# A kernel of attention and experts: the search's constants in two streams, and one more expert's first layer by seven products of sums

## The chip, the cores and the metric

One core of a Trainium2 chip runs the whole program. The time is the core's device time in microseconds for one execution, as the median of three runs. Everything is float32 unless the code says otherwise.

## The reference

The first half is a linear attention with decay (4 batches, 8 heads, 768 steps, 48 columns a head). Its output, 3072 rows of 384, goes to a mixture of eight experts in which each expert takes exactly 384 rows.

```python
for t in range(S):
    kt, vt, rt = (k[:, :, t], v[:, :, t], r[:, :, t])
    cur = np.einsum('bhd,bhe->bhde', u[None] * kt, vt)
    y[:, :, t] = np.einsum('bhd,bhde->bhe', rt, state + cur)
    state = w[None, :, :, None] * state + np.einsum('bhd,bhe->bhde', kt, vt)
...
logits = x @ w_gate
flat = logits.flatten()
order = np.argsort(-flat)
for idx in order:
    tok, e = (int(idx) // E, int(idx) % E)
    if assigned[tok] >= 0 or counts[e] >= cap:
        continue
    assigned[tok] = e
    counts[e] += 1
...
    h = np.maximum(x[mask] @ w1[e], 0.0)
    out[mask] = h @ w2[e]
```

w1 of an expert is 384 x 1024, w2 is 1024 x 384.

## The kernel before, in words

**Attention** (`Mild`). A unit is 128 steps of one batch; there are 24, four batches a chunk. Units are worked in an order written out by hand in `Mild.run`: in the turn of unit n, PE multiplies the pairs of unit n + 1, turns k and r of unit n + 2 (`kT_ps`, `rT_ps`, line 460) and makes the outputs of unit n (`y_ps`, line 547). VectorE sums `rk` into `dd` (450), scales r (479) and copies the masked pairs into `AT` (514). ACT writes the diagonal of `AT` from `dd` (497, eight writes a unit), copies the outputs out (`x`, 566) and the transposed rows (`xr`, 606). GpSimd multiplies the keys (438) and `rk` (444, 445) and decays the state (532). Each fourth unit also makes the gate's logits. Every engine takes its instructions strictly in the order in which they were written.

**The constants.** The search for the experts' rows needs some twenty small tables. `Assignment.constants` is a generator that issues one instruction a step, GpSimd's and VectorE's mixed, in the order in which the text stands. `Mild.run` takes six steps of it behind each unit from n = 3 on and the rest, if any, behind unit 13. `iota_i`, `own_i`, `number_i` and `by_digit` are written by GpSimd and read by VectorE in the next steps. `digit_15`, `digits`, `steps` and `top` are read only by `surely`, the search that is used in the other arm of the branch at line 2051, which is for inputs that the fast search could not settle.

**The search.** For each expert in turn `likely_steps` finds, with three rounds of counts, the threshold and the rows. A round is a chain between two engines: VectorE writes `ind`, PE counts (978), VectorE writes `own`, `cnt` and `wide`, PE adds up with `ones_h` (989), VectorE reads `most`. After the third, `acc` marks the rows, PE adds them up (`st_ps`, 1105), VectorE makes `place`, `row`, `oh` and `vals`, PE lists (`some_ps` 1450, `list_ps` 1469), and `tok` names the rows. GpSimd then gathers them (1558) and SP loads w1 and w2 of that expert (1551). The search of one expert runs beside the products of the expert two before it, and its small products stand among the large ones in PE's order.

**The experts.** In `Experts.run` an expert is two layers. The expert numbered 0 takes 256 rows early, under the end of attention; 1 to 7 take 384 rows each, and a last turn the remaining 128. The first layer is either plain (`hidden`, `h_ps` at line 1683: 8 blocks of F by 3 of D, 384 columns a product) or by seven (`hidden_by_seven`, line 1660: the 2 x 2 blocks of the first 256 columns of x and of w1 by seven products of sums, with the products of the last 128 columns added in the same banks; 192 columns a product). By seven needs four sums of w1 (`weight_sums`, `first_T`, line 1607), five of the rows (`row_sums`, `first_S`, line 1618) and six additions of kept products (`kept_P`, 1652). The weight sums are made beside the expert before, issued after its first sum `S`; the row sums after the search's `acc`. There is one buffer for each sum. Second layers of experts 1 to 5 are by seven over two thirds of the rows (`seven`, `pa_ps`, `pb_ps`, `pc_ps`, line 1757, with S sums of the hidden rows and T sums of w2 at 1732) and plain over the rest (`o_ps`, 1818); those of 6 and 7 are by fifteen products. Every product in float32 is two passes on PE, and the trace counts passes.

In this part the order on each engine is made by the compiler's scheduler from its own costs, not by hand, so that an added instruction moves others.

Of the kernel before, what the change touches and what calls it, by code (L numbers as in the profile page):

```python
# [13 lines left out]
I32 = mybir.dt.int32  # L14
# [4 lines left out]
ALU = mybir.AluOpType  # L19
AX = mybir.AxisListType  # L20
PSUM = bass.MemoryType.PSUM

NEG = -3.4028234663852886e38
# [253 lines left out]
class Mild:  # L277
# [343 lines left out]
    def run(self, step):  # L621
# [38 lines left out]
        for n in range(N):  # L660
# [66 lines left out]
            if n > 2:  # L727
                for _ in range(6):
                    next(chores, None)
# [8 lines left out]
class Assignment:  # L738
# [24 lines left out]
    def __init__(self, ctx, tc, ML, CAP, C):  # L763
# [22 lines left out]
        new("iota", [128, 128])  # L786
# [14 lines left out]
        new("iota_lo", [128, 128], I32)  # L801
# [23 lines left out]
    def constants(self):  # L825
        nc = self.nc
        NT, E, ND, G, LO = self.NT, self.E, self.ND, self.G, self.LO
        nc.gpsimd.memset(self.ones, 1.0)
        yield
        nc.gpsimd.memset(self.ones_h, 1.0)  # L830
        yield

        nc.gpsimd.memset(self.rest_of, -1.0)
        yield
        nc.gpsimd.affine_select(out=self.rest_of, in_=self.rest_of, compare_op=ALU.is_ge, fill=0.0,
                                base=0, pattern=[[-1, 128]], channel_multiplier=1)
        yield
        nc.gpsimd.memset(self.ones_t, 1.0)
        yield
        nc.gpsimd.memset(self.neg, NEG)  # L840
        yield


        nc.gpsimd.memset(self.by_digit, 1.0)
        yield
        for sign in (1, -1):
            nc.gpsimd.affine_select(out=self.by_digit, in_=self.by_digit, compare_op=ALU.is_ge, fill=0.0, base=0,
                                    pattern=[[-G * sign, ND], [-sign, G]], channel_multiplier=sign)
            yield
        with nc.allow_low_precision(reason="zero or one"):  # L850
            nc.vector.tensor_reduce(out=self.digit_of[:, :, 0], in_=self.by_digit, axis=AX.X, op=ALU.add)
        yield
        nc.vector.tensor_copy(self.digit_of[:, :, 1:E], self.digit_of[:, :, 0:1].to_broadcast([128, ND, E - 1]))
        yield
        nc.vector.tensor_reduce(out=self.same, in_=self.by_digit.rearrange("p d g -> p g d"), axis=AX.X, op=ALU.add)
        yield
        for g in range(3):
            nc.gpsimd.iota(self.from_digit[:, g], pattern=[[ND ** (2 - g), ND], [0, G]],
                           base=(ND ** 2 - ND ** 3, ND, 0)[g], channel_multiplier=0)
            yield  # L860
        Q, NC = 128 // LO, self.CAP // 128
        nc.gpsimd.iota(self.lo_of, pattern=[[1, LO], [0, Q]], base=0, channel_multiplier=0)
        yield
        nc.gpsimd.iota(self.hi_of, pattern=[[1, NC * Q], [0, Q]], base=Q, channel_multiplier=0)
        yield
        nc.vector.tensor_copy(self.digit_15, self.digit_of)
        yield
        nc.vector.memset(self.digit_15[:, ND - 1:ND, :], 0.0)
        yield

        nc.gpsimd.memset(self.quarter, 1.0)
        yield
        for sign, base in ((1, 0), (-1, LO - 1)):
            nc.gpsimd.affine_select(out=self.quarter, in_=self.quarter, compare_op=ALU.is_ge, fill=0.0, base=base,
                                    pattern=[[-LO * sign, Q]], channel_multiplier=sign)
            yield

        nc.gpsimd.iota(self.iota_i, pattern=[[1, 128]], base=0, channel_multiplier=0)
        yield
        nc.vector.tensor_copy(self.iota, self.iota_i)  # L880
        yield
        nc.gpsimd.iota(self.own_i, pattern=[[0, 1]], base=0, channel_multiplier=1)
        yield
        nc.vector.tensor_single_scalar(out=self.own_q, in_=self.own_i, scalar=Q - 1, op=ALU.bitwise_and)
        yield
        nc.vector.tensor_copy(self.own_lo, self.own_q)
        yield
        nc.vector.tensor_scalar(out=self.fourth, in0=self.iota[:, 0:Q], scalar1=self.own_lo, scalar2=None,
                                op0=ALU.is_equal)
        yield  # L890
        nc.vector.tensor_single_scalar(out=self.own_q, in_=self.own_i, scalar=Q.bit_length() - 1,
                                       op=ALU.arith_shift_right)
        yield
        nc.vector.tensor_copy(self.own_lo, self.own_q)
        yield
        nc.vector.tensor_single_scalar(out=self.iota_lo, in_=self.iota_i, scalar=LO - 1, op=ALU.bitwise_and)
        yield
        nc.vector.tensor_scalar(out=self.alike, in0=self.iota_lo, scalar1=self.own_lo, scalar2=None, op0=ALU.is_equal)
        yield
        nc.vector.tensor_scalar(out=self.first_e, in0=self.iota[:, 0:E], scalar1=-1.0, scalar2=float(E),  # L900
                                op0=ALU.mult, op1=ALU.add)
        yield
        nc.vector.tensor_copy(self.first_b, self.first_e)
        yield

        nc.gpsimd.iota(self.number_i, pattern=[[128, NT]], base=-64 * NT, channel_multiplier=1)
        yield
        nc.vector.tensor_copy(self.number, self.number_i)
        yield

        nc.gpsimd.iota(self.digits, pattern=[[1, ND]], base=1, channel_multiplier=0)
        yield
        for g in range(8):
            nc.vector.tensor_single_scalar(out=self.steps[:, g, :], in_=self.digits, scalar=28 - 4 * g,
                                           op=ALU.logical_shift_left)
            yield
# [3 lines left out]
        yield  # L920
        nc.vector.tensor_single_scalar(out=self.top[:, 7:ND - 1], in_=self.steps[:, 0, 7:ND - 1],
                                       scalar=-2147483648, op=ALU.bitwise_xor)
        yield
        nc.vector.tensor_copy(self.top[:, ND - 1:ND], self.top[:, ND - 2:ND - 1])
        yield
        nc.gpsimd.memset(self.taken, 0.0)
        yield
        nc.gpsimd.memset(self.star_place, 0)
        yield
        nc.gpsimd.memset(self.last, float(E * (E - 1) // 2))  # L930
        yield
# [560 lines left out]
def rwkv5_eagle_then_base_layer_balanced(  # L1492
# [34 lines left out]
    class Experts:  # L1527
# [299 lines left out]
        FIRST_BY_SEVEN = 3, 6, 7  # L1827
# [269 lines left out]
```

## Time and profile before

| | us |
|---|---|
| median of 3 runs | 389.97 (389.80 to 390.12) |
| the profiled execution | 389.62 |
| its span, first to last instruction | 387.9 |
| PE busy | 371.6 |
| VectorE (DVE) busy | 268.2 |
| ACT busy | 187.1 |
| GpSimd (POOL) busy | 142.2 |
| first layer of expert 2, plain, starts | 186.4 |
| first layer of expert 3, by seven, starts | 218.0 |

PE is busy for 96% of the span and its granted clock is 0.989 over the whole. In rows of the timeline the first number is the start, the second the length, then the engine, the line, the operation and the tiles (out<-in), the shapes and how many were merged; in brackets stands the idle time of the engine before it and who ended it. PE's rows merge passes of one form, and their lengths contain the modelled drain, so rates are taken from one start to the next.

### The profile page before, as it was taken

The page shows a single profiled execution, that of the slowest core. Times are in us where ns is not written, and L with a number is a line of the kernel's source. Part 1 is how long each engine was busy: PE and PEld are TensorE (multiplying, and loading weights), DVE is VectorE, ACT ScalarE, POOL GpSimd, SP SyncE. Part 2 cuts the span into 40 slices and gives each one's busy share as a digit, 9 for nine tenths or more (in the row PEclk, how much of TensorE's full clock was granted, in tenths as well). Part 3 has the DMA queues.
Part 4 walks back from the last instruction along what each step waited for, and adds up shares of the span by engine and source line. Part 5 has one row for each costly group of instructions (what it writes and reads, how often), then busy time and mean ns, then how long its engine had stood idle before and what let it go on. Part 6 is the DMA issues. An engine that isn't in the chain of part 4 may idle for free. (4 is left out here: it accounts for less than half of the span.)

```text
span 387.9 us, 9795 instructions
## 1 busy us (share of the span) xinstructions
PE 371.6 (96%) x3729; PEld 300.7 (78%) x3729; DVE 268.2 (69%) x940; ACT 187.1 (48%) x468; POOL 142.2 (37%) x175
## 2 busy tenths in 40 slices
PE   7799999999999999999999999999999999999992
PEld 5677878888887775778569799658756889989991
DVE  6655777666887568877649948869367964995530
ACT  4898879888885312225223544322222535535220
POOL 7878877867762005032121221202202322060030
PEclk9899999999999999999999999999999999999997
DMA  7969977777593236473382770408308564690110
GB/s 147 208 133 198 199 165 167 170 169 160 121 327 90 98 130 275 129 280 81 95 333 55 169 285 22 103 0 293 134 23 291 175 235 192 84 365 22 24 63 28
DMA packets 108136, 60.51 MB, mean 156 GB/s; under 512 B 90032, under 2 KB 102320, under 8 KB 108080
## 3 DMA queue, kind: packets, MB, share of 16 engines
q1 hardware_dynamic: 104736, 50.35, 47.5%
q0 software_dynamic: 3104, 9.44, 6.5%
q8 instruction: 31, 0.51, 0.6%
q14 instruction: 25, 0.20, 0.2%
q10 hardware_dynamic: 240, 0.00, 0.0%
HBM read 47.20 MB, written 9.44 MB: 146 GB/s over the span
## 5 line engine op out<-in xcount | busy, mean ns | idle before, releaser
L1683 PE MATMUL h_ps<-xT,w 128*128 128x384 f32 (+1 forms) x264 | 72.7, 427 | 0.0
L497 ACT ACTIVATE AT<-ident,dd 128x128 f32<-128x128 f32 x192 | 59.6, 392 | 4.5 <-DVE dd L450 4.5
L1683 PEld LDWEIGHTS h_ps<-xT,w 128*128 128x128 f32 x264 | 42.0, 191 | 19.7 <-issue 2.3
L1812 POOL DMA_INDIRECT out_dram<-o_all,to x16 | 21.1, 1318 | 92.2 <-DVE o_all L1800 41.0
L1558 POOL DMA_INDIRECT xg<-x_rows,tok x22 | 22.1, 1006 | 84.1 <-DVE own_c L1484 32.7
L1686 ACT ACTIVATE hid<-h_ps 128x384 f32<-128x384 f32 (+1 forms) x40 | 17.9, 448 | 54.8 <-PE h_ps L1683 51.5
L514 DVE COPY_PREDICATED AT<-mask,g_ps 64x512 f32<-64x512 uint8 (+1 forms) x48 | 32.4, 724 | 9.7 <-PE g_ps L507 9.2
L1818 PE MATMUL o_ps<-w,hid 128*128 128x384 f32 x96 | 33.3, 491 | 0.2 <-DVE o_all L1747 0.2
L438 POOL TENSOR_TENSOR kss<-krs,wk 128x384 f32<-128x384 f32 x24 | 24.3, 1014 | 11.6 <-DVE krs L342 7.4
L507 PE MATMUL g_ps<-rT,kT 48*64 48x128 f32 (+1 forms) x768 | 26.9, 258 | 1.4 <-DVE AT L514 0.7
L547 PE MATMUL y_ps<-AT,vts 128*64 128x128 f32 x384 | 26.6, 282 | 0.0
L1818 PEld LDWEIGHTS o_ps<-w,hid 128*128 128x128 f32 x96 | 17.5, 190 | 10.3 <-DVE o_all L1747 0.5
L445 POOL TENSOR_TENSOR rk<-rk,u_bc 128x384 f32<-128x384 f32 x24 | 24.1, 1005 | 1.9
L507 PEld LDWEIGHTS g_ps<-rT,kT 48*64 48x64 f32 x768 | 21.0, 134 | 4.7 <-PE unread_ps L420 0.9
L444 POOL TENSOR_TENSOR rk<-krs 128x384 f32<-128x384 f32 x24 | 24.5, 1021 | 0.0
L547 PEld LDWEIGHTS y_ps<-AT,vts 128*64 128x64 f32 x384 | 21.3, 141 | 1.2 <-issue 0.5
L450 DVE TENSOR_REDUCE dd<-rk 128x8 f32<-128x384 f32 x24 | 13.1, 545 | 7.3 <-POOL rk L445 7.2
L479 DVE TENSOR_TENSOR rT<-rT_ps,WR 112x512 f32<-112x512 f32 x23 | 15.7, 681 | 2.4 <-PE rT_ps L460 2.4
L566 ACT COPY x<-y_ps 128x512 f32<-128x512 f32 x24 | 14.0, 585 | 5.9 <-PE y_ps L547 5.0
L1648 ACT ACTIVATE hid<-kept_P 128x384 f32<-128x384 f32 x18 | 9.4, 523 | 15.2 <-DVE kept_P L1652 14.9
L460 PE MATMUL rT_ps<-ident,krs 128*112 128x128 f32 x96 | 14.9, 274 | 0.7 <-ACT krs L346 0.7
L1757 PE MATMUL pa_ps<-T,S 128*128 128x192 f32 x80 | 15.5, 331 | 0.0
(346 smaller groups left out, 828.9 us busy)
## 6 DMA issues: line engine op xcount, KB each, us to landing
w<-in_moe_w_dram SPq DMA_DIRECT2D x18, 1536.0 KB, 8.6
krs<-in_k_dram SPq DMA_DIRECT2D x24, 192.0 KB, 3.5
krs<-in_r_dram SPq DMA_DIRECT2D x24, 192.0 KB, 3.7
vts<-in_v_dram SPq DMA_DIRECT2D x24, 192.0 KB, 3.6
x_rows<-xr SPq DMA_DIRECT2D x24, 192.0 KB, 2.5
xg<-x_rows,tok POOLq DMA_INDIRECT x22, 4.3
xg<-xg SPq DMA_TRANSPOSE x16, 2.8
out_dram<-o_all,to POOLq DMA_INDIRECT x16, 3.0
```

The costliest lines, as they stand in the source:

```text
L438: self.nc.gpsimd.tensor_mul(self.kss[:, n % self.NS].rearrange("p (g h) d -> p g h d", g=2)[:, :, :, 0:D], src, self.wk.rearrange("p (g h) ...
L444: nc.gpsimd.tensor_mul(rk, self.krs[:, n % self.NK, 1, 0:H, 0:D], self.krs[:, n % self.NK, 0, 0:H, 0:D])
L445: nc.gpsimd.tensor_mul(rk, rk, self.u_bc)
L497: nc.scalar.mul(AT[:, z, a, :], self.ident, dd[:, h:h + 1])
L507: nc.tensor.matmul(g_ps[ts(i, PD), z, a, i * PD:], kT[rows, a, ts(i, PD)], rT[rows, a, i * PD:], start=True, stop=True)
L514: nc.vector.copy_predicated(out=AT[keys, :, :, steps], mask=mask, data=g_ps[keys, :, :, steps])
L547: nc.tensor.matmul(yv[q * PD:(q + 1) * PD, o // 2, o % 2, :], lhsT, rhs, start=(o // 2, q) not in seen, stop=stop, skip_group_check=True)
L1558: nc.gpsimd.indirect_dma_start(out=xg[:, c, :], out_offset=None, in_=x_dram[0:within, :], in_offset=bass.IndirectOffsetOnAxis(ap=tok[:, c: ...
L1683: nc.tensor.matmul(h_ps[j][:, at], w1[:, f, ts(j, 128)], xT[:, f, at], start=(f == 0), stop=(f == KD - 1))
L1686: self.copied = nc.scalar.activation(hid[:, j, 0:m], h_ps[j][:, 0:m], AF.Relu)
L1812: nc.gpsimd.indirect_dma_start(out=to, out_offset=bass.IndirectOffsetOnAxis(ap=tok, axis=0), in_=o_sb, in_offset=None)
L1818: nc.tensor.matmul(o_ps, hid[:, j, ts(c, 128)], w2[:, j, :], start=(j == 0), stop=(j == KF - 1))
```

## The change

The constants become two generators, `by_gpsimd` and `by_vector`. `constants` takes six steps of GpSimd's alone, and from then on one of each in every step. GpSimd's order starts with what VectorE reads. `Mild.run` takes four steps behind a unit instead of six. `digit_15`, `digits`, `steps` and `top` are made in `general_constants`, which `restart` calls at the start of the other arm. `iota` is 8 columns instead of 128, and `iota_lo` is written over `iota_i`. Second, expert 2 joins the experts whose first layer is by seven.

```diff
@@ Mild.run
             if n > 2:
-                for _ in range(6):
+                for _ in range(4):
                     next(chores, None)
@@ Assignment
-        new("iota", [128, 128])
+        new("iota", [128, E])
...
-        new("iota_lo", [128, 128], I32)
     def constants(self):
+        first, then = self.by_gpsimd(), self.by_vector()
+        for _ in range(6):
+            yield next(first)
+        while True:
+            done = [next(part, self) is self for part in (then, first)]
+            if all(done):
+                return
+            yield
+
+    def by_gpsimd(self):
...
+        yield nc.gpsimd.iota(self.iota_i, pattern=[[1, 128]], base=0, channel_multiplier=0)
+        yield nc.gpsimd.iota(self.own_i, pattern=[[0, 1]], base=0, channel_multiplier=1)
+        yield nc.gpsimd.memset(self.by_digit, 1.0)
         for sign in (1, -1):
...
+        yield nc.gpsimd.iota(self.number_i, pattern=[[128, NT]], base=-64 * NT, channel_multiplier=1)
...
+    def by_vector(self):
...
+        yield nc.vector.tensor_copy(self.iota, self.iota_i[:, 0:E])
+        yield nc.vector.tensor_single_scalar(out=self.own_q, in_=self.own_i, scalar=Q - 1, op=ALU.bitwise_and)
...
+    def general_constants(self):
+        nc, E, ND = self.nc, self.E, self.ND
         nc.vector.tensor_copy(self.digit_15, self.digit_of)
-        yield
         nc.vector.memset(self.digit_15[:, ND - 1:ND, :], 0.0)
...
         nc.gpsimd.iota(self.digits, pattern=[[1, ND]], base=1, channel_multiplier=0)
-        yield
         for g in range(8):
             nc.vector.tensor_single_scalar(out=self.steps[:, g, :], in_=self.digits, scalar=28 - 4 * g,
                                            op=ALU.logical_shift_left)
-            yield
...
     def restart(self):
+        self.general_constants()
@@ Experts
-        FIRST_BY_SEVEN = 3, 6, 7
+        FIRST_BY_SEVEN = 2, 3, 6, 7
```

How the instructions stand on the engines, at the places of which the prediction speaks (rows of before with its lines, rows of the change with the lines of the changed text):

VectorE in attention, before, at the end of unit 6's turn: `digit` is the copy that is read only in the other arm, `iota_i` GpSimd's table, `dd` the row sum for ACT.

```order
L531 TENSOR_TENSOR states<-states,kv_ps 128x4x48
L868 MEMSET digit_71 128x4
L880 CAST iota<-iota_i 128x128
L342 COPY krs<-krs 128x2x48
L450 TENSOR_REDUCE dd<-rk 128x8
L479 TENSOR_TENSOR rT<-rT_ps,WR 112x512
```

And now, in the same place:

```order
L531 TENSOR_TENSOR states<-states,kv_ps 128x4x48
L877 TENSOR_SCALAR iota_i<-iota_i 128x128
L878 TENSOR_SCALAR alike<-iota_i,own_lo 128x128
L880 TENSOR_SCALAR first_e<-iota 128x8
L882 CAST first_b<-first_e 128x8
L342 COPY krs<-krs 128x2x48
L450 TENSOR_REDUCE dd<-rk 128x8
L479 TENSOR_TENSOR rT<-rT_ps,WR 112x512
```

The copy of `iota` has moved two turns up, and GpSimd's `iota_i`, which stood in the turn of the reader, is now the first constant behind unit 3.

VectorE in the second layer of expert 1, before: `em` belongs to the search, S are sums of the hidden rows, `own`, `cnt` and `wide` the search's answer to a count.

```order
L1075 TENSOR_REDUCE em<-eq 128x24
L1732 TENSOR_TENSOR S_3154<-hid 128x512
L1732 TENSOR_TENSOR S_3156<-S_3154,hid 128x512
L955 TENSOR_TENSOR own<-counts,same 128x64
L1732 TENSOR_TENSOR S_3158<-hid,S_3156 128x512
L986 TENSOR_REDUCE cnt<-own 128x8
L1747 TENSOR_TENSOR o_all<-kept_P_3167,pc_ps 128x192
L955 TENSOR_TENSOR wide<-digit_of,cnt 128x128
```

And now:

```order
L1047 TENSOR_REDUCE em<-eq 128x24
L1579 TENSOR_TENSOR first_T_3154<-w_3062 128x512
L1704 TENSOR_TENSOR S_3139<-hid 128x512
L1579 TENSOR_TENSOR first_T_3156<-w_3062,first_T_3154 128x512
L1704 TENSOR_TENSOR S_3141<-S_3139,hid 128x512
L1579 TENSOR_TENSOR first_T_3158<-w_3062 128x512
L1704 TENSOR_TENSOR S_3143<-hid,S_3141 128x512
L1579 TENSOR_TENSOR first_T_3160<-w_3062,first_T_3156 128x512
L1719 TENSOR_TENSOR o_all<-kept_P_3152,pc_ps 128x192
L926 TENSOR_TENSOR own<-counts,same 128x64
```

The four weight sums of expert 2 stand among the S sums, and `own` behind all of them; `cnt` and `wide` follow among the sums of w2.

PE from the end of expert 1's second layer into expert 2's first, now (`h_ps`, `hc_ps` and `hb_ps` are banks of the first layer by seven; before, the plain products `h_ps` of 384 columns stood here, two ahead of `ones_h` and three behind it):

```order
L1632 MATMUL h_ps<-xT,w_3062 128x192 x2
L1632 MATMUL hc_ps<-xT,w_3062 128x192
L960 LDWEIGHTS ones_h
L960 MATMUL counts<-wide,ones_h 128x128
L1632 MATMUL hc_ps<-xT,w_3062 128x192 x3
L1632 MATMUL hb_ps<-xT,w_3062 128x192 x2
L1077 LDWEIGHTS ones
L1077 MATMUL st_ps<-acc,ones 128x24
```

Between the last count (`ones_h`) and `st_ps` stand five products of 192 columns, where before three of 384 stood.

More of the change, by code (lines that the diff above doesn't have):

```diff
@@ L850, in constants @@
-        with nc.allow_low_precision(reason="zero or one"):
[L851 to L865, printed above, removed]
+        Q, NC = 128 // LO, self.CAP // 128
+        yield nc.gpsimd.iota(self.iota_i, pattern=[[1, 128]], base=0, channel_multiplier=0)
+        yield nc.gpsimd.iota(self.own_i, pattern=[[0, 1]], base=0, channel_multiplier=1)
+        yield nc.gpsimd.memset(self.by_digit, 1.0)
@@ new lines, in by_gpsimd @@
+        for sign in (1, -1):
+            yield nc.gpsimd.affine_select(out=self.by_digit, in_=self.by_digit, compare_op=ALU.is_ge, fill=0.0, base=0,
+                                          pattern=[[-G * sign, ND], [-sign, G]], channel_multiplier=sign)
+        yield nc.gpsimd.iota(self.number_i, pattern=[[128, NT]], base=-64 * NT, channel_multiplier=1)
+        yield nc.gpsimd.memset(self.quarter, 1.0)
+        for sign, base in ((1, 0), (-1, LO - 1)):
+            yield nc.gpsimd.affine_select(out=self.quarter, in_=self.quarter, compare_op=ALU.is_ge, fill=0.0, base=base,
+                                          pattern=[[-LO * sign, Q]], channel_multiplier=sign)
@@ new lines, in by_gpsimd @@
+        yield nc.gpsimd.iota(self.lo_of, pattern=[[1, LO], [0, Q]], base=0, channel_multiplier=0)
+        yield nc.gpsimd.iota(self.hi_of, pattern=[[1, NC * Q], [0, Q]], base=Q, channel_multiplier=0)
+        for g in range(3):
+            yield nc.gpsimd.iota(self.from_digit[:, g], pattern=[[ND ** (2 - g), ND], [0, G]],
+                                 base=(ND ** 2 - ND ** 3, ND, 0)[g], channel_multiplier=0)
+        yield nc.gpsimd.memset(self.ones, 1.0)
+        yield nc.gpsimd.memset(self.ones_h, 1.0)
@@ new lines, in by_gpsimd @@
+        yield nc.gpsimd.memset(self.rest_of, -1.0)
+        yield nc.gpsimd.affine_select(out=self.rest_of, in_=self.rest_of, compare_op=ALU.is_ge, fill=0.0,
+                                      base=0, pattern=[[-1, 128]], channel_multiplier=1)
+        yield nc.gpsimd.memset(self.ones_t, 1.0)
+        yield nc.gpsimd.memset(self.neg, NEG)
+        yield nc.gpsimd.memset(self.taken, 0.0)
+        yield nc.gpsimd.memset(self.star_place, 0)
+        yield nc.gpsimd.memset(self.last, float(E * (E - 1) // 2))
@@ new lines, in by_vector @@
+    def by_vector(self):
+        nc = self.nc
+        NT, E, ND, LO = self.NT, self.E, self.ND, self.LO
+        Q = 128 // LO
+        yield nc.vector.tensor_copy(self.iota, self.iota_i[:, 0:E])
+        yield nc.vector.tensor_single_scalar(out=self.own_q, in_=self.own_i, scalar=Q - 1, op=ALU.bitwise_and)
+        yield nc.vector.tensor_copy(self.own_lo, self.own_q)
+        yield nc.vector.tensor_scalar(out=self.fourth, in0=self.iota[:, 0:Q], scalar1=self.own_lo, scalar2=None,
+                                      op0=ALU.is_equal)
+        yield nc.vector.tensor_single_scalar(out=self.own_q, in_=self.own_i, scalar=Q.bit_length() - 1,
+                                             op=ALU.arith_shift_right)
+        yield nc.vector.tensor_copy(self.own_lo, self.own_q)
+        yield nc.vector.tensor_single_scalar(out=self.iota_i, in_=self.iota_i, scalar=LO - 1, op=ALU.bitwise_and)
+        yield nc.vector.tensor_scalar(out=self.alike, in0=self.iota_i, scalar1=self.own_lo, scalar2=None,
+                                      op0=ALU.is_equal)
+        yield nc.vector.tensor_scalar(out=self.first_e, in0=self.iota, scalar1=-1.0, scalar2=float(E),
+                                      op0=ALU.mult, op1=ALU.add)
+        yield nc.vector.tensor_copy(self.first_b, self.first_e)
+        yield nc.vector.tensor_copy(self.number, self.number_i)
+        with nc.allow_low_precision(reason="zero or one"):
+            yield nc.vector.tensor_reduce(out=self.digit_of[:, :, 0], in_=self.by_digit, axis=AX.X, op=ALU.add)
+        yield nc.vector.tensor_copy(self.digit_of[:, :, 1:E], self.digit_of[:, :, 0:1].to_broadcast([128, ND, E - 1]))
+        yield nc.vector.tensor_reduce(out=self.same, in_=self.by_digit.rearrange("p d g -> p g d"), axis=AX.X,
+                                      op=ALU.add)
@@ L866, in constants @@
+    def general_constants(self):
+        nc, E, ND = self.nc, self.E, self.ND
         nc.vector.tensor_copy(self.digit_15, self.digit_of)
-        yield
         nc.vector.memset(self.digit_15[:, ND - 1:ND, :], 0.0)
[L869 to L909, printed above, removed]
         nc.gpsimd.iota(self.digits, pattern=[[1, ND]], base=1, channel_multiplier=0)
-        yield
```

25 lines of the change are left out of this document (removed).

## The prediction

> **What bounds the kernel now.** I read the page's busy times first, then the table by stretch.
>
> ```profile
> PE 371.6 (96%) x3729; PEld 300.7 (78%) x3729; DVE 268.2 (69%) x940; ACT 187.1 (48%) x468; POOL 142.2 (37%) x175
> 30.00:66.00 36.00, 34.99 (x734) 29.61 (x734) 24.83 (x64) 29.48 (x89) 29.75 (x51) 1.00 0.82 180
> 186.40:202.60 16.20, 16.20 (x63) 9.38 (x62) 10.39 (x56) 3.91 (x8) 3.87 (x4) 1.00 0.66 243
> 202.60:218.00 15.40, 15.37 (x88) 12.48 (x86) 13.32 (x46) 6.83 (x12) 2.44 (x2) 1.00 0.40 65
> 218.00:233.40 15.40, 15.18 (x102) 14.77 (x101) 10.20 (x49) 6.87 (x14) 4.01 (x4) 1.00 0.69 256
> ```
>
> The columns of the last four rows are the stretch, its length, and the busy time of PE, PEld, DVE, ACT and POOL, then clock, DMA share and GB/s. PE is busy almost throughout at full clock in all four. So two things shorten the run: fewer PE passes, or a PE wait taken away. Work taken off another engine counts only where PE waits for it. The last three rows are the first layer of expert 2 (plain), its second layer, and the first layer of expert 3 (by seven). PE waits little there, but it follows one written order, and the search's small products stand in it: a late VectorE shows up as a PE wait.
>
> **First edit: the constants.** The attention units between 30 and 66 us hold one sizeable PE wait, and its chain is plain in the timeline:
>
> ```profile
> 48.93 0.24 POOL L878 IOTA iota_i<- 128x128 int32 x1
> 49.21 0.23 DVE L880 CAST iota<-iota_i 128x128 f32<-128x128 int32 x1 [2.52 <-POOL iota_i L878]
> 49.47 0.55 DVE L450 TENSOR_REDUCE dd<-rk 128x8 f32<-128x384 f32 x1
> 50.05 2.45 ACT L497 ACTIVATE AT<-ident,dd 128x128 f32<-128x128 f32 x8 [1.27 <-DVE dd L450]
> 52.41 0.56 ACT L566 COPY x<-y_ps 128x512 f32<-128x512 f32 x1
> 53.02 0.60 PE L597 MATMUL x_ps<-ident,x 112*128 112x112 f32 x4 [0.78 <-ACT x L566]
> 53.29 0.15 DVE L884 TENSOR_SCALAR own_q<-own_i 128x1 int32<-128x1 int32 x1 [1.18 <-POOL own_i L882]
> ```
>
> VectorE stood 2.52 us at a constant, because GpSimd writes `iota_i` only after its own attention work. Behind it in the queue are the row sum `dd`, the eight diagonal writes on ACT, the copy of x on ACT, and the PE transpose that waits 0.78 us. In the new order `iota_i` and `own_i` are GpSimd's first constants, a unit ahead of their readers, and `by_digit` is three units ahead. So the waits of 2.52 and 1.18 us go. What the wait is worth on PE is read from the start of each unit's r transposes:
>
> ```profile
> 51.64 0.27 PE L460 MATMUL rT_ps<-ident,krs 128*112 128x128 f32 x1
> 58.28 0.38 PE L460 MATMUL rT_ps<-ident,krs 128*112 128x128 f32 x2
> 71.46 0.27 PE L460 MATMUL rT_ps<-ident,krs 128*112 128x128 f32 x1
> 77.11 0.27 PE L460 MATMUL rT_ps<-ident,krs 128*112 128x128 f32 x1
> 90.73 0.27 PE L460 MATMUL rT_ps<-ident,krs 128*112 128x128 f32 x1
> 96.38 0.27 PE L460 MATMUL rT_ps<-ident,krs 128*112 128x128 f32 x1
> ```
>
> The unit with the wait took 58.28 - 51.64 = 6.64 us; its two likes later took 5.65 (77.11 - 71.46 and 96.38 - 90.73). That is 0.99 us to gain. The three units behind the waiting one took 13.18 (to 71.46), the three behind a clean one 13.62 (77.11 to 90.73): up to 0.44 may be given back, since ACT, at 30 of 36 us, comes out of the wait with slack that it won't have. I take 0.8, with bounds of 0.5 and 1.1 (the upper one for small waits near 40 us). Fewer operations are worth nothing on their own:
>
> ```profile
> L914 DVE TENSOR_SCALAR steps<-digits 128x16 int32<-128x16 int32 x8 | 1.2, 212 | 0.7 <-POOL digits L911 0.7
> ```
>
> These 1.2 us, the copy into `digit_15` and the `top` writes leave VectorE, which has 11 us free of 36 there, and go to an arm that this run doesn't enter. Were VectorE full, all of it would count. The earlier constants put under 1.2 us on GpSimd in each unit, as now.
>
> **Second edit: expert 2's first layer by seven.** The PE saving comes from the starts of runs of one form:
>
> ```profile
> 194.77 7.99 PE L1683 MATMUL h_ps<-xT,w 128*128 128x384 f32 x24
> 202.59 0.25 PE L978 MATMUL counts<-prop,ind 128*128 128x64 bf16 x3
> 218.73 1.46 PE L1660 MATMUL hc_ps<-xT,w 128*128 128x192 f32 x8
> 220.03 0.81 PE L1660 MATMUL hb_ps<-xT,w 128*128 128x192 f32 x4
> ```
>
> A pass of 384 columns takes 7.82/24 = 0.326 us, one of 192 takes 1.30/8 = 0.163. Each product is two passes. Plain: 8 blocks x 3 x 2 = 48 passes, 15.6 us. By seven: 11 pairs x 2 x 2 x 2 = 88 passes, 14.3 us. That saves 1.30. With the search's products and waits between, the two stages above differ by 16.2 - 15.4 = 0.8, which is how I start; the 0.5 between is restarts of the narrow runs and one wait for `vals` (below).
>
> The Trainium skill, TensorE: Matmul & The Clock Gate, section Back-to-back issue gap, speaks against this: it puts the spacing in a stream of weight loads and matmuls at about 81 ns for 128 columns and 131 for 512, so narrow products cost more per column. By a straight line between these (an estimate) 88 x 89 ns against 48 x 114 would be 2.4 us slower, and this edit would come to +3.2 (the -0.5 below without the 1.30 saved, and 2.4 more). The trace disagrees: 0.163 is half of 0.326.
>
> The work that comes with it is on VectorE: four weight sums, five row sums, six additions into `kept_P`; ACT gets six more copies, in a stage where it was busy 3.91 of 16.20 us. What VectorE's queue does around the weight sums:
>
> ```profile
> 169.21 0.35 DVE L1075 TENSOR_REDUCE em<-eq 128x24 f32<-128x192 bf16 x1
> 172.04 0.69 DVE L1732 TENSOR_TENSOR S<-hid 128x512 f32<-128x512 f32 x1 [2.48 <-ACT hid L1686]
> 174.09 1.46 PE L1757 MATMUL pb_ps<-T,S 128*128 128x192 f32 x8
> 161.33 0.37 SPq L1551 DMA_DIRECT2D w<-in_moe_w_dram  x1
> w<-in_moe_w_dram SPq DMA_DIRECT2D x1, 1536.0 KB, 10.0
> 200.96 1.29 DVE L1607 TENSOR_TENSOR first_T<-w 128x512 f32<-128x512 f32 x2 [4.45 <-DMA w<-in_moe_w_dram]
> 203.32 0.69 DVE L1732 TENSOR_TENSOR S<-hid 128x512 f32<-128x512 f32 x1 [0.46 <-ACT hid L1686]
> 203.93 0.68 DVE L1607 TENSOR_TENSOR first_T<-w,first_T 128x512 f32<-128x512 f32 x1
> ```
>
> The first weight sum now stands between `em` and S. It waits for w1, issued at 161.33 and landed 10.0 later, at 171.3. At 0.61 a sum (203.32 to 203.93) it is done as S becomes ready at 172.04. The other three alternate with the S sums, so S2 and S4 start 0.6 and 1.2 later; the products that read them follow 1.3 us apart from 174.09 on, so they stay ahead. Behind them wait the search's `own`, `cnt`, `wide`: about 2.5 us later, but their product has been moved four products down PE's queue, so no more than 0.05 shows. No DMA moves to another queue; the loads are the same.
>
> Three waits are new and one goes. Their rows:
>
> ```profile
> 187.81 0.22 PE L989 MATMUL counts<-wide,ones_h 128*128 128x128 f16 x1
> 189.48 0.24 DVE L1100 SCALAR_TENSOR_TENSOR acc<-em,fmax,past 128x24 bf16<-128x24 f32 x1
> 189.85 0.18 PE L1105 MATMUL st_ps<-acc,ones 128*128 128x24 bf16 x1
> 218.15 0.35 DVE L1618 TENSOR_TENSOR first_S<-xT 128x192 f32<-128x192 f32 x1
> 222.03 0.31 PE L1450 MATMUL some_ps<-vals,row 128*128 128x48 f16 x6 [0.22 <-DVE vals L955]
> 178.10 0.49 PE L1757 MATMUL pa_ps<-T,S 128*128 128x192 f32 x2
> 178.62 0.26 PE L978 MATMUL counts<-prop,ind 128*128 128x64 bf16 x3
> ```
>
> (a) From the last count of a search to its `st_ps` VectorE needs between 1.91 us (187.81 to the end of `acc` at 189.72) and 2.04 (to `st_ps`, which came behind other products); I take 1.96, nearer the first, since PE was not waiting. The new order has ten narrow passes there, 1.63, and 0.15 for the count and the restart: a wait of 0.18, in expert 2 and again in expert 3, 0.36. (b) The last row sum now follows `vals`; it is 0.35 long (218.15), while PE has only the short run of `some_ps` before the product that reads it: I take 0.15, between 0 and 0.35, in each of the two, 0.3. The wait for `vals` itself (0.22 at 222.03) stays as it was in expert 3 and is counted for expert 2 in the 15.4. (c) In expert 2's second layer expert 3's weight sums can no longer run early, since the tiles are still being read. Eight sums at 0.61 from the first S on (203.32, 0.73 behind PE's 202.59), 0.25 for `wide`: 5.85 us, where PE arrives at 5.7: 0.1. (d) On the other side two waits go: 178.62 - 178.10 is 0.52 for two passes of 0.163, so PE waited 0.19 for `ind`, and the same stands in the next expert; both counts have moved: -0.37. Sum: -0.8 + 0.05 + 0.36 + 0.3 + 0.1 - 0.37 = -0.4. Adding the same steps up position by position through both experts gives -0.55, as restarts partly fall into waits; I take -0.5. Bounds: -1.3 (no new wait) and +0.7 (each of the search's six counts in the two experts 0.2 later, as `ind` and `vals` are today).
>
> **The sum.** -0.8 - 0.5 = -1.3 on the profiled execution's 389.62 us, so 388.3. That execution is 0.35 under the median of 389.97: 388.65 in the timed runs, and I say 388.6. About 0.2% (0.78 us) is what a measurement of this kernel can tell from no change.
>
> **The rivals.**
> A. Both gains in full: 1.1 and 1.3 give 387.6. For it: 192-column passes do run at half. Against it: VectorE at 13.32 of 15.40 us between.
> B. One of the two is lost: PE's written order assumes other delays than the chip has, and each of the six counts waits 0.1 to 0.2 more, or ACT hands the attention gain back in the next units. 389.3 to 389.9, no change. For it: `vals` already comes 0.22 late. Against it: the wait at 49.21 can't return.
> C. Slower: w1 for expert 2 lands late. VectorE runs in order, and its head is then a load. For it: expert 3's first weight sum sat 4.45 us for its load at 200.96. If expert 2's did, it would start at 174.0, S at 174.6, and the product at 174.09 would start 1.2 late; the search's `wide` would come at 180.9 where PE, 1.2 late, wants it at 179.5: 1.4 more. 2.6 lost, 1.3 gained: 389.97 + 1.3 = 391.3. It decides from about 1.4 us of lateness on. Against it: that is a landing of 11.4, and
>
> ```profile
> DMA to landing us min/median/max: 6.3/8.6/11.3
> L1660 PEld LDWEIGHTS hc_ps<-xT,w 128*128 128x128 f32 x48 | 8.0, 190 | 0.0
> ```
>
> no load of weights took longer than 11.3.
> D. Narrow products bound by their weight loads: at 190 ns a pass (second row) 88 passes take 16.7 us, 1.1 more than the plain 15.6. The forecast without the 1.30 and with 1.1 more is 388.65 + 2.4 = 391.05. Against it: three experts' runs at 0.163. The Trainium skill's rule above would act here in this way.
>
> **Chances.** Forecast 0.63, A 0.14, B 0.17, C 0.04, D 0.02. The likeliest's own range is 388.0 to 389.2. I give 387.5 to 389.7, which takes in A and most of B and leaves out C and D. Faster by over 0.2% (under 389.2): most of the forecast, A, and a little of B: 0.76. Within 0.2%: 0.19. Slower: 0.05.
>
> **What would show it.** Right: no VectorE wait for a GpSimd constant, the unit that took 6.64 us at about 5.7, and everything after attention 0.8 earlier; expert 2's first layer at about 15.5 us instead of 16.2, with `st_ps` waiting some 0.2; the first weight sum starting at about the landing of w1, before S. Wrong: PE waits over 0.5 us between the two experts, a first weight sum that starts more than 1.4 us behind S's readiness, or units after attention's gate that lengthen by what the one lost.

## The result, and the profile after

The changed kernel takes 388.15 us (median; 387.69 to 388.72), the kernel before 389.97 beside it: a ratio of 0.9948, 95% interval 0.9929 to 0.9967. That is 1.8 us less; the prediction said 388.6 and 1.3 less. The sign, the range and the two places of the gain are right. The sizes are not, and one effect that nobody looked for takes a part of the gain back. The profiled execution took 387.69 us, span 386.0.

The busy times of the page, and the table by stretch of the kernel after (columns as in the prediction; the second row is the attention, the last three are expert 2's first layer, its second layer, and expert 3's first layer):

```profile
PE 369.8 (96%) x3769; PEld 305.2 (79%) x3769; DVE 273.2 (71%) x942; ACT 190.6 (49%) x474; POOL 142.7 (37%) x174
```

```profile
0.00:20.00 20.00, 15.30 (x199) 12.45 (x201) 14.66 (x36) 13.69 (x44) 16.17 (x26) 1.00 0.88 170
30.00:66.00 36.00, 35.84 (x758) 30.81 (x758) 25.17 (x60) 30.64 (x90) 31.13 (x55) 1.00 0.87 189
184.70:200.20 15.50, 15.38 (x104) 14.79 (x103) 12.31 (x63) 6.97 (x14) 3.88 (x4) 1.00 0.71 254
200.20:215.30 15.10, 15.10 (x84) 12.39 (x83) 13.02 (x33) 6.93 (x12) 2.76 (x2) 1.00 0.35 68
215.30:230.90 15.60, 15.47 (x103) 14.87 (x102) 12.46 (x65) 6.98 (x14) 3.86 (x4) 1.00 0.72 252
```

PE's 34.99 of 36 us in the attention are now 35.84: a wait has gone. Expert 2's first layer has come down from 16.2 to 15.5 us. The first row needs its counterpart of the kernel before:

```profile
0.00:20.00 20.00, 15.38 (x184) 12.60 (x185) 13.68 (x33) 12.72 (x42) 16.16 (x26) 0.91 0.91 178
```

The mean granted clock there was 0.91 before and is 1.00 after, and 1.2 us of the difference between these two executions arise before 20 us. It is no work of the change: the second profiled execution of the kernel before (below) shows 0.91 again, but the two kernels below that have the same instructions and only other addresses have 1.00 there, and over the timed executions the mean clock goes from 0.989 to 0.998 for the kernel before and from 0.990 to 0.997 for the changed one. So from here on I compare stages behind this stretch, and stages of two executions of the kernel before.

The starts of the attention's units after the change, and the constants' rows:

```profile
45.78 0.60 PE L460 MATMUL rT_ps<-ident,krs 128*112 128x128 f32 x4
50.13 0.60 PE L460 MATMUL rT_ps<-ident,krs 128*112 128x128 f32 x4
55.77 0.60 PE L460 MATMUL rT_ps<-ident,krs 128*112 128x128 f32 x4
```

```profile
31.17 0.24 POOL L838 IOTA iota_i<- 128x128 int32 x1
35.86 0.17 DVE L869 CAST iota<-iota_i 128x8 f32<-128x8 int32 x1
35.93 0.15 DVE L870 TENSOR_SCALAR own_q<-own_i 128x1 int32<-128x1 int32 x1
```

The unit that took 6.64 us takes 55.77 - 50.13 = 5.64. `iota_i` starts 4.7 us ahead of its reader, and neither reader waits.

### The profile page after: what moved, and what is told of

The parts are those of the page before. It is cut to its first block, busy times and chain, and to the rows that moved or that the text cites. A ratio compares the mean times of both kernels' runs of the same rounds, so it can differ in the third digit from the quotient of the medians.

```text
span 386.0 us, 9900 instructions
## 1 busy us (share of the span) xinstructions
PE 369.8 (96%) x3769; PEld 305.2 (79%) x3769; DVE 273.2 (71%) x942; ACT 190.6 (49%) x474; POOL 142.7 (37%) x174
## 4 chain that ended last, share of the span: by engine, by line
PE 58%; issue 16%; DVE 9%; POOL 6%; DMA 4%; ACT 4%; POOLq 1%; another core or an unknown queue 0%; SPq 0%; DVEq 0%
PE h_ps L1655 8%; PE o_ps L1790 5%; PE y_ps L547 5%; PE pa_ps L1729 5%; PE h_ps L1632 5%; PE hb_ps L1632 4%; PE g_ps L507 4%; DMA xg<-x_rows,tok 3%; PE pb_ps L1729 3%; PE e_h_ps L1899 3%; ACT AT L497 2%; PE x_ps L597 2%; PE kv_ps L526 2%; PE kT_ps L460 2%; PE lg_ps L577 2%
## 5 line engine op out<-in xcount | busy, mean ns | idle before, releaser
L1655 PE MATMUL h_ps<-xT,w 128*128 128x384 f32 (+1 forms) x216 | 56.7, 412 | 0.1
L1655 PEld LDWEIGHTS h_ps<-xT,w 128*128 128x128 f32 x216 | 33.4, 191 | 14.6 <-issue 1.9
L514 DVE COPY_PREDICATED AT<-mask,g_ps 64x512 f32<-64x512 uint8 (+1 forms) x48 | 32.5, 727 | 11.9 <-PE g_ps L507 10.4
L1658 ACT ACTIVATE hid<-h_ps 128x384 f32<-128x384 f32 (+1 forms) x32 | 13.9, 437 | 42.9 <-PE h_ps L1655 40.9
L547 PE MATMUL y_ps<-AT,vts 128*64 128x128 f32 x384 | 25.7, 276 | 0.0
L1620 ACT ACTIVATE hid<-kept_P 128x384 f32<-128x384 f32 x24 | 12.6, 523 | 17.4 <-DVE kept_P L1624 16.9
L1763 PE MATMUL p_ps<-W,H 128*128 128x128 f32 x128 | 15.3, 275 | 0.0
```

Source lines behind the costliest of these rows:

```text
L514: nc.vector.copy_predicated(out=AT[keys, :, :, steps], mask=mask, data=g_ps[keys, :, :, steps])
L547: nc.tensor.matmul(yv[q * PD:(q + 1) * PD, o // 2, o % 2, :], lhsT, rhs, start=(o // 2, q) not in seen, stop=stop, skip_group_check=True)
L1655: nc.tensor.matmul(h_ps[j][:, at], w1[:, f, ts(j, 128)], xT[:, f, at], start=(f == 0), stop=(f == KD - 1))
```

## The experiments

Each kernel's profiled execution is cut at the same six places: the start of the unit near 23 us, the last attention unit, and the starts of expert 1's first layer, expert 3's first layer, expert 3's second layer and the last second layer. Times in us, from the starts of PE's rows in the timeline; "packet" is the median length in ns of the 1,536 DMA packets of 4,608 bytes (gathered and scattered rows), taken from the trace's packet records; "timed" is the median against the kernel before of the same comparison, with the ratio's interval. What each kernel is stands in the experiments below the table.

| kernel | attention | to expert 1 | to expert 3 | its first layer | rest | sum | packet | timed |
|---|---|---|---|---|---|---|---|---|
| before, again | 91.91 | 38.84 | 64.42 | 15.31 | 142.55 | 353.03 | 178 | -0.07 (0.998-1.0003) |
| two constants first | 90.65 | 38.77 | 64.41 | 15.23 | 142.54 | 351.60 | 178 | -1.37 (0.995-0.9983) |
| the same, fewer operations | 90.65 | 38.86 | 64.41 | 15.47 | 142.53 | 351.91 | 178 | -1.28 (0.9955-0.9982) |
| first edit, tiles aligned | 90.64 | 38.85 | 64.41 | 15.49 | 142.58 | 351.97 | 178 | -0.91 (0.996-0.9986) |
| first edit | 90.62 | 39.02 | 64.41 | 16.09 | 142.83 | 352.97 | 195 | -0.05 (0.999-1.0013) |
| first edit, operations kept | 90.61 | 39.24 | 64.70 | 16.18 | 142.99 | 353.72 | 194 | +0.03 (0.9992-1.0019) |
| before, tiles moved 32 bytes | 91.92 | 39.20 | 64.67 | 15.75 | 143.48 | 355.02 | 194 | +0.81 (1.0012-1.0043) |
| before, tiles moved 64 bytes | 91.90 | 39.13 | 65.41 | 15.77 | 143.36 | 355.56 | 195 | +0.98 (1.0009-1.0043) |
| second edit | 92.00 | 38.85 | 63.22 | 15.52 | 142.61 | 352.20 | 178 | -1.49 (0.9939-0.9973) |
| whole change | 90.63 | 39.02 | 63.22 | 15.52 | 142.94 | 351.33 | 195 | -1.82 (0.9929-0.9967) |
| whole change, tiles aligned | 90.66 | 38.80 | 63.22 | 15.51 | 142.50 | 350.69 | 178 | -2.55 (0.9911-0.9947) |
| two first and second edit | 90.66 | 38.87 | 63.21 | 15.52 | 142.52 | 350.78 | 178 | -2.84 (0.9908-0.9953) |

**The kernel before, again.** No edit.

> The kernel before, once more, for the clock of each execution. Its first trace has the tensor engine's clock granted at one half for 3.4 us (14.5 to 17.9 us), mean clock 0.989; the trace after the change has no such stretch (0.997), and 1.2 us of the difference between the two traces arise there. Theory 'chance': the stretch falls on some executions of either kernel; then some executions here show about 0.997 and are about 1.2 us shorter (388.6 to 388.8). Rival 'the kernel': the kernel before has it nearly always; then all executions show about 0.989 to 0.990, at 389.6 to 390.2.

Neither theory holds as written. The clock's mean was 0.993 to 0.998 in this comparison, and 0.989 to 0.997 in the executions of the kernel before beside it, but the time follows it only loosely: several executions at 0.995 took 389.2 to 389.6 us, those at 0.997 about 390.0. One reason may be that the mean counts the time ahead of the trace's first clock record as full: that record comes between 4.2 and 10.8 us in the profiles here, which doesn't show in the mean. The trace gives a better picture: behind 23 us it needs 353.03 us, 0.98 more than the first profile's 352.05. Of that 0.83 lie between the last attention unit and expert 1 (38.84 against 38.01), most of it between 124 and 128 us; every later execution has 38.8 or more there. So the profile on which the prediction stood was a lucky one there and an unlucky one at the clock.

**The first edit alone.**

```
-        FIRST_BY_SEVEN = 2, 3, 6, 7
+        FIRST_BY_SEVEN = 3, 6, 7        (in the changed kernel)
```

> First edit alone: the constants in two streams, expert 2's first layer left plain. The prediction: 0.8 us under the kernel before (0.5 to 1.1). Theory from the traces: the attention gains 1.3 us (1.0 in the unit of the 2.52 us wait, 0.3 two units earlier) and nothing is given back up to 113 us; 0.3 to 0.7 may be lost where the tensor engine then meets gathered rows that are not there (the wait of 0.26 for xg at the first whole expert), so 0.6 to 1.3 under at the same clock. If the missing half-clock stretch comes with this edit, 1.2 us more: 1.8 to 2.5 under.

390.01 us: no gain. The attention is 1.29 us shorter, as in the whole change, and 1.2 are lost behind it: 0.18 in front of expert 1, 0.78 in expert 3's first layer, 0.28 later. The timeline of this kernel at expert 3's first layer shows the place:

```profile
217.63 0.36 DVE L1590 TENSOR_TENSOR first_S<-xT 128x192 f32<-128x192 f32 x1 [0.88 <-ACT xT L1565]
221.89 0.31 PE L1422 MATMUL some_ps<-vals,row 128*128 128x48 f16 x6 [0.95 <-DVE vals L926]
```

VectorE stands at expert 3's row sums for xT, which comes from a DMA transpose; behind them in its queue the search makes `vals`, and PE waits 0.95 us for that, where it waited 0.17 to 0.22 in the kernel before. A part of a kernel that the edit doesn't touch, 150 us behind it, had become slower.

**The second edit alone.**

```
-        FIRST_BY_SEVEN = 3, 6, 7
+        FIRST_BY_SEVEN = 2, 3, 6, 7     (in the kernel before)
```

> Second edit alone: expert 2's first layer by seven, the constants as before. The prediction: 0.5 us under the kernel before (bounds 1.3 under, 0.7 over). Theory from the traces: from the start of expert 1's second layer to the start of expert 3's second layer 1.0 us is gained (0.2, 0.7, 0.1), and 0.0 to 0.4 of it lost at a later gather: 0.6 to 1.0 under at the same clock. Rival: the gain of the second edit shows only because the first has shifted the gathers; then under 0.3.

1.49 us under by the timed runs, 0.83 by the stages: 1.20 less between experts 1 and 3, 0.21 more in expert 3's first layer. The rival is out. The interval (1.1 to 2.4) lies above the trace's figure; its profiled execution was the slowest of the kernel, and one of the three that have the half-clock stretch near 14.5 us. I take the trace's 1.0 as the gain and leave the rest open.

**Two constants first, nothing removed.**

```
     def constants(self):
+        nc.gpsimd.iota(self.iota_i, ...); yield
+        nc.gpsimd.iota(self.own_i, ...); yield
         nc.gpsimd.memset(self.ones, 1.0)
...
-        nc.gpsimd.iota(self.iota_i, ...); yield
-        nc.gpsimd.iota(self.own_i, ...); yield
```

> Of the first edit only this: the two constants that VectorE waited for (iota_i and own_i) become GpSimd's first, everything else is as before, no operation is removed. Theory: the 2.52 us wait is all of the unit's loss, so that unit takes 5.65 us instead of 6.64 and the kernel is 0.9 to 1.0 under the one before at the same clock, 0.3 less than the whole first edit in the attention (unit two before it unchanged, 4.63). Rival: the removed operations and the later constants count too; then the unit stays above 6.0 us and the gain is under 0.6.

Moving two instructions gives the attention the whole gain, and the kernel 1.37 us:

```profile
42.08 0.60 PE L460 MATMUL rT_ps<-ident,krs 128*112 128x128 f32 x4
46.44 0.60 PE L460 MATMUL rT_ps<-ident,krs 128*112 128x128 f32 x4
50.80 0.60 PE L460 MATMUL rT_ps<-ident,krs 128*112 128x128 f32 x4
56.44 0.60 PE L460 MATMUL rT_ps<-ident,krs 128*112 128x128 f32 x4
```

The unit takes 5.64 us (56.44 - 50.80), and the one two before it became 0.3 shorter as well (46.44 - 42.08 = 4.36; 4.63 in the kernel before), which I had not expected of this kernel; what shortens that one was not separated. So the fourteen operations that the first edit takes away are worth nothing here, and something in that edit costs 1.3 us. Two things differ: VectorE's code is shorter, which may move the places where code is loaded; and the constants' pool is 992 bytes smaller (`iota` 512 to 32, `iota_lo` 512 to none). Every later tile lies behind that pool: the first `xg` at address 66048 before, at 65056 after. The next three kernels separate the two.

**The first edit with its operations kept.**

```
-        self.general_constants()            (in restart)
+        yield from self.general_constants() (at the end of by_vector)
```

> The first edit alone (expert 2 plain), but with the fourteen operations that it moves to the restart arm put back among the constants, so that VectorE executes as many operations as before; the smaller tile iota and the missing iota_lo stay. The first edit alone came out at 390.0 although its attention is 1.3 us shorter; 0.75 of that was lost in expert 3's first layer, where VectorE stood 0.88 us at the row sums for xT, and about 0.5 at two gathers. Theory 'code': fewer operations shift the places at which 8 KB of code are loaded, one into expert 3's transposes; then this kernel is at 388.6 to 388.8 and its gather packets of 4608 B still take 193 ns. Theory 'address': 992 bytes less in the constants' pool put all later tiles 32 bytes off a multiple of 64, and packets get longer (178 to 193 ns); then this kernel stays at 389.9 to 390.1.

**Two first, with the operations moved away.** The reverse: before's tiles, fewer operations.

```
     def restart(self):
+        self.general_constants()            (digit_15, digits, steps, top: no longer in constants)
```

> The kernel with only iota_i and own_i first (388.7), and the fourteen operations moved to the restart arm as the change does; the tiles stay as in the kernel before, so all later ones at multiples of 64 bytes. Theory 'code': 389.8 to 390.1, expert 3's first layer 16.1 us. Theory 'address': 388.6 to 388.8, expert 3's first layer 15.4 us, packets of 4608 B at 178 ns.

**The first edit with aligned tiles.**

```
-        new("iota", [128, E])
+        new("iota", [128, 256])
```

> The first edit alone (expert 2 plain) with iota made 992 bytes longer, so that all later tiles are at multiples of 64 bytes again; nothing else differs from the kernel that took 390.0. Theory 'address': 388.6 to 388.8, packets of 4608 B at 178 ns. Theory 'code': 389.9 to 390.1.

The three agree. With the small tiles the gain is lost whether the operations are there or not (390.38 beside 390.35 for the kernel before); with the tiles back at their places it is there without the operations (389.07, 389.44, against the same 390.35; these medians lie 0.3 to 0.7 above what was expected, as that of the kernel before does). "Code" is out as the main cause; it may be worth the 0.2 by which expert 3's first layer is longer in both kernels with fewer operations (15.47, 15.49 against 15.23, 15.31), which wasn't separated. The DMA rows of the page, first edit and then the same with aligned tiles; the columns of the queue are packets, MB, share, those of the gather its median time to landing:

```profile
q0 software_dynamic: 3104, 9.44, 7.2%
...
xg<-x_rows,tok POOLq DMA_INDIRECT x22, 4.8
```

```profile
q0 software_dynamic: 3104, 9.44, 6.6%
...
xg<-x_rows,tok POOLq DMA_INDIRECT x22, 4.4
```

The same packets and bytes take longer, and a gathered row block lands 0.4 us later. By the packet records, 4,608 bytes take 195 instead of 178 ns, 4,096 bytes 164 instead of 159, 3,072 bytes 129 to 131 instead of 121. At expert 3's row sums the aligned kernel waits like this:

```profile
216.29 0.36 DVE L1590 TENSOR_TENSOR first_S<-xT 128x192 f32<-128x192 f32 x1 [0.33 <-ACT xT L1565]
...
220.50 0.31 PE L1422 MATMUL some_ps<-vals,row 128*128 128x48 f16 x6 [0.36 <-DVE vals L926]
```

0.33 and 0.36 instead of 0.88 and 0.95.

**The whole change with aligned tiles.** The same line in the changed kernel.

> The changed kernel with the same 992 bytes given back to iota. In its trace the two gathers cost 0.23 and 0.31 us more than in the kernel before. Theory 'address': 387.4 to 387.7, packets of 4608 B at 178 ns, no wait for xg over 0.1 us at the first whole expert. Theory 'code': within 0.2 us of the changed kernel's 388.15.

387.8 us, ratio 0.993. The attention, expert 2 and expert 3's first layer are those of the whole change to 0.03 us; 0.66 less lie in the two other stages (38.80 against 39.02, 142.50 against 142.94). The whole change's own wait, which this kernel doesn't have:

```profile
PE xT_ps L1545 <- DMA xg<-x_rows,tok: 0.3, 1, 0.3
```

**The kernel before, with all later tiles moved by 32 and by 64 bytes.** No instruction differs.

```
-        new("iota", [128, 128])
+        new("iota", [128, 136])         (and 144)
```

> The kernel before with one tile of the constants' pool (iota) 32 bytes longer, nothing else: all later tiles lie 32 bytes off a multiple of 64, no instruction is added, removed or moved. Theory 'address': packets of 4608 B take 193 ns instead of 178, expert 3's first layer 16.1 us instead of 15.3, the gathers of experts 1 and 5 are waited for; 0.8 to 2.0 us slower than the kernel before, as the two kernels with the first edit alone lost 1.2 and 2.0 behind the attention. Rival (the loss needs the new order of the constants): within 0.2 us of the kernel before.

> The kernel before with iota 64 bytes longer: later tiles move by the same kind of step but stay at multiples of 64 bytes, while they leave multiples of 512. Theory 'address, 64 bytes': packets at 178 ns, time within 0.2 us of the kernel before. Rivals: a boundary of 128 or more bytes counts (then slower by 0.8 to 2.0), or any shift of the tiles does.

Both are slower, by 0.81 and 0.98 us (ratios 1.0027 and 1.0026), with packets of 194 and 195 ns. So the address alone does it, and my 64 bytes were wrong: 64 off costs as much as 32. It is the transfers that get longer, not the engines' work: over the instructions that stand equally often in the three traces, VectorE's durations add up to 320.2 us in the kernel before (second execution) and to 319.7 and 319.6 with the tiles moved, ACT's to 213.5, 213.7 and 213.5. 66048 is 258 x 256 and also 129 x 512; which boundary beyond 64 counts these runs don't tell. The Trainium skill, DMA: Bandwidth & Descriptors, section How a descriptor splits into AXI transactions, says that a descriptor is cut into transactions of 256 bytes that must start at multiples of 256, so that one which starts elsewhere begins at the boundary below its start and fetches bytes that it doesn't use. By that rule 66048 is aligned and the starts 32 and 64 bytes off are not, and the packets of 3,072 to 4,608 bytes agree with it. The 12,288 packets of 1,536 bytes do not: their median is 65 ns in every kernel here, though three quarters of them fill w2's tiles, which have moved with the rest. So the rule fits the direction, and what sets the sizes stays open. I had not looked at the tiles' sizes in the diff with this in mind.

In the second of the two the loss shows at a third place, expert 2's second layer. Its rows, and then those of the second execution of the kernel before:

```profile
191.28 1.03 SPq L1551 DMA_DIRECT2D w<-in_moe_w_dram  x2
...
203.17 1.29 DVE L1607 TENSOR_TENSOR first_T<-w 128x512 f32<-128x512 f32 x2 [6.15 <-DMA w<-in_moe_w_dram]
...
208.25 0.22 PE L989 MATMUL counts<-wide,ones_h 128*128 128x128 f16 x1 [0.91 <-DVE wide L955]
```

```profile
191.58 1.03 SPq L1551 DMA_DIRECT2D w<-in_moe_w_dram  x2
...
201.85 1.29 DVE L1607 TENSOR_TENSOR first_T<-w 128x512 f32<-128x512 f32 x2 [4.53 <-DMA w<-in_moe_w_dram]
```

Expert 3's weights land 11.9 us behind their issue instead of 10.3 (11.3 was the longest load in the first profile), and the search's `wide` waits in VectorE's queue behind their sums. This is rival C's mechanism, one expert later than I had put it. It is seen in one execution, the slowest of its ten.

**Two first and the second edit.** Two instructions moved and one number added, the tiles at before's places.

> The kernel before with only iota_i and own_i first, and expert 2's first layer by seven: the smallest edit that should hold all that the change gains. The single kernels came out 1.3 and 1.5 us under the kernel before of their day, the whole change with the tiles at multiples of 64 bytes 2.5 under. Theory 'address': the same 2.3 to 2.6 under (387.5 to 387.9), packets at 178 ns. Rival (the rest of the first edit is worth something): 0.3 or more above the whole change with aligned tiles.

387.71 us, ratio 0.9931: all of the gain, from the smallest edit. It and the whole change with aligned tiles can't be told apart, and both beat the kernel before and, by the stages (350.8 and 350.7 against 351.3), the changed one; by the timed runs alone the intervals overlap.

**Expert 4 by seven, too.**

```
-        FIRST_BY_SEVEN = 2, 3, 6, 7
+        FIRST_BY_SEVEN = 2, 3, 4, 6, 7  (whole change, tiles aligned)
```

> The whole change with aligned tiles, and expert 4's first layer by seven as well (2, 3, 4, 6, 7). By the measured terms of expert 2: 1.3 us less on the tensor engine, 0.2 to 0.5 given back in waits of the written order: 0.8 to 1.1 under the whole change with aligned tiles, near 386.8. Rival: expert 3's second layer, which then has to make expert 4's sums while the search runs at its full rate (six counts in expert 4's first layer), waits for VectorE: no gain.

400.36 us, ten slower. The rival was right about VectorE, though not about the place: it is in expert 4's own first layer, and far larger than a lost gain.

```profile
253.70 0.22 PE L960 MATMUL counts<-wide,ones_h 128*128 128x128 f16 x1 [1.17 <-DVE wide L926]
255.37 0.26 PE L949 MATMUL counts<-prop,ind 128*128 128x64 bf16 x3 [1.46 <-DVE ind L926]
256.52 0.24 PE L960 MATMUL counts<-wide,ones_h 128*128 128x128 f16 x1 [0.89 <-DVE wide L926]
258.23 0.34 PE L949 MATMUL counts<-prop,ind 128*128 128x64 bf16 x3 [1.46 <-DVE ind L926]
```

```profile
246.20:256.50 10.30, 6.53 (x43) 5.59 (x42) 8.95 (x49) 2.48 (x5) 0.97 (x1) 1.00 0.06 21
256.60:266.80 10.20, 4.20 (x22) 3.49 (x22) 7.59 (x45) 0.48 (x1) 0.00 (x0) 0.50 0.18 49
```

PE's order has the six counts one behind another with no product between them, so each of the last five waits out VectorE's whole chain (0.9 to 1.5 us). PE is busy for only 0.53 of the last 3.41 us of that, and then the granted clock falls to 0.50 for ten more (last row). Why the order comes out so was not looked into.

## Why the prediction was right or wrong

- **The wait for `iota_i`** (right). Moving two GpSimd instructions removes it and takes the unit from 6.64 to 5.64 us, as its likes said (5.65). The removed operations are worth nothing, as said.
- **"Up to 0.44 may be given back ... I take 0.8"** (mis-sized). Nothing is given back: from the unit at 55.77 to the last one at 113.07 the trace after takes 57.30, the trace before 57.31. To the 1.00 come 0.27 from a unit near 46 us: 1.27 in all. I had taken three units against three others as a sign of slack on ACT; the difference between them was a matter of which units they were. The same three after the change take 13.18 again.
- **The second edit, -0.5** (mis-sized in step (b)). The start was good: 15.4 for expert 2's first layer, and with the waits below 15.4 + 0.23 + 0.21 - 0.37 = 15.5, as measured. Step (b) let the old wait for `vals` stand and put 0.15 for the last row sum on top, in both experts. The old wait is 0.37 by the starts in the prediction's window (two passes from 221.33 on, `some_ps` at 222.03; the 0.22 in its row counts from the modelled end of the second pass). In fact the new wait, 0.21, takes the place of the old one: with the row sums spread behind the search's steps `vals` is in time, and only the last row sum is late. So (b) is not +0.3 but 2 x (0.21 - 0.37) = -0.32. With that, and with (a) to (d) as measured below, -0.8 + 0.46 - 0.32 + 0.14 - 0.38 = -0.9; the stages show -1.20 between the experts and +0.21 in expert 3's first layer, -1.0.
- **The waits one by one** were nearly all as said. The rows of the kernel after:

```profile
186.87 0.81 PE L1632 MATMUL hb_ps<-xT,w 128*128 128x192 f32 x4
187.75 0.17 PE L1077 MATMUL st_ps<-acc,ones 128*128 128x24 bf16 x1
...
190.48 0.81 PE L1632 MATMUL hb_ps<-first_S,first_T 128*128 128x192 f32 x4
191.15 0.31 PE L1422 MATMUL some_ps<-vals,row 128*128 128x48 f16 x6
191.51 0.89 PE L1632 MATMUL h_ps<-first_S,first_T 128*128 128x192 f32 x4
...
205.52 0.49 PE L1729 MATMUL pb_ps<-w,S 128*128 128x192 f32 x2
205.99 0.22 PE L960 MATMUL counts<-wide,ones_h 128*128 128x128 f16 x1
```

  (a) `st_ps` comes 0.88 behind four passes of 0.163: a wait of 0.23, said 0.18. (b) From `some_ps` to the product that reads the last row sum it is 0.36 instead of 0.15: 0.21 in each expert, said 0.15; it replaces a wait of 0.37 (above). (c) `wide`: 0.47 behind two passes, 0.14, said 0.1. (d) Both waits for `ind` are gone, as said.
- **The first weight sum** (right): it starts as w1 lands, before S.

```profile
167.71 0.35 DVE L1047 TENSOR_REDUCE em<-eq 128x24 f32<-128x192 bf16 x1
169.91 0.69 DVE L1579 TENSOR_TENSOR first_T<-w 128x512 f32<-128x512 f32 x1 [1.85 <-DMA w<-in_moe_w_dram]
170.54 0.69 DVE L1704 TENSOR_TENSOR S<-hid 128x512 f32<-128x512 f32 x1
```

- **What was missing**: that a smaller tile moves all later ones. In the whole change this costs 0.64 us by the stages; alone with the first edit it costs 1.00 and so all of the gain. The second edit hides the 0.60 of it in expert 3's first layer, which then takes 15.52 and 15.51 with the two layouts; probably because the row sums now stand between and behind the search's steps instead of ahead of them, which was not tried by itself.
- **The sum**: -1.27 - 1.0 + 0.64 = -1.6, against -1.82 timed and -1.70 by the stages. I said -1.3, from two gains each 0.5 too small and a loss that I didn't see. The timed time fell within the range for partly wrong reasons.
- **Rivals**: A, both gains in full at 387.6, is what the aligned kernels do (387.7, 387.8). B's outcome, one gain lost, is what the first edit does alone, by another cause than named. C did not decide in expert 2. D is out: expert 2's narrow passes run at 0.163 as elsewhere, and the Trainium skill's rule on the issue gap, which the prediction weighed, doesn't fit this kernel.

## What to carry to other kernels

A tile made smaller "on the side" moves every tile allocated behind it: look at where the DMA buffers then start, keep that at the multiple that it had (here 66048; 32 and 64 bytes off both cost), and test a clean-up apart from the edit that should gain. When two stages are compared to price a third, list which waits each of them already contains before adding any. A wait that ends on a constant or another early product of an idle engine is worth moving first: two instructions gave all of the first edit's gain.

## What the runs showed of the hardware that was not expected

- **Start addresses of DMA buffers in SBUF**: 32 or 64 bytes off 66048 lengthen a packet of 4,608 bytes from 178 to 195 ns, of 4,096 from 159 to 164, of 3,072 from 121 to about 130, leave those of 1,536 at 65, and cost this kernel 0.7 to 1.0 us timed (0.6 to 2.5 by the stages of single executions), depending on which waits stand at the edge.
- **The clock early in the run** differs between executions of one kernel: in some the trace's clock record has full clock from 4.3 us on with a stretch of 3.4 us at one half from 14.5 us, in some full clock throughout from 4.6 to 5.0 us on, in some full clock only from 9 to 11 us on. The unit that starts at 22.4 us in the second case starts at 22.7 to 23.1 in the third and at 23.6 in the first.
- **Half clock after waits**: in the kernel with expert 4 by seven, PE was busy for 0.53 of the 3.41 us up to 256.58 us; the clock was 0.50 for the next 10.24 us and came back behind 3.41 us in which PE was busy for 3.24. The early half-clock stretch looks alike: in the three executions that have it PE was busy for about 1.7 of the 3.41 us ahead of it. Counted in steps of 3.41 us from the first full clock on, and apart from these two stretches, no step of any profile has under 1.98 until the last 10 us of the run. Busy time alone doesn't decide, for near the end of one run 1.42 of 3.41 us were followed by full clock. In all fourteen profiles the changes of the clock lie whole multiples of 3.41 us apart, so the same waits can fall into one step or be divided between two; that this makes the difference between executions is likely, and not shown. The Trainium skill, TensorE: Matmul & The Clock Gate, Part 1, section What's actually happening, tells of a gate that halves the clock by activity in windows of about 3.4 us; the stretches here, 3.4 and three times that, agree with it.
